# A gated mix of a state-space layer and an FFN: B turned by transposing transfers, ten FFN tiles ahead of the first Bu, one run of second FFN products

## The chip, the cores and the metric

The kernel runs on one core of one Trainium2 chip. The metric is the device time of one execution in microseconds (us). The core has five engines with instruction streams of their own: TensorE (PE in the profile, its weight loads PEld), VectorE (DVE), ScalarE (ACT), GpSimd (POOL) and SyncE (SP), which here only issues transfers (DMAs). KB is 1024 bytes.

## The reference

For each of 2048 tokens x has 448 features. Two branches are computed from it and mixed by a gate:

```python
g = sigmoid((x * gate_w).sum(-1, keepdims=True))
# branch a: a diagonal complex recurrence over the tokens
dt = exp(log_dt); Lam_bar = exp(dt * Lam)
B_bar = ((Lam_bar - 1) / Lam)[:, None] * (B_re + 1j * B_im)
Bu = x @ B_bar.T                        # 448 complex states for each token
h[t] = Lam_bar * h[t - 1] + Bu[t]
a = 2 * (h @ (C_re + 1j * C_im).T).real + x * Dskip
# branch b: an FFN
b = silu(x @ w1) @ w2                   # 448 -> 1792 -> 448
out = g * a + (1 - g) * b
```

## The kernel before

The tokens are cut into four chunks of 512. Four kinds of product on TensorE make up nearly all of its time:

- F(tc): the first FFN product of chunk tc, 14 tiles of 128 hidden features by 512 tokens. ScalarE evicts each from PSUM through Silu into `aT[tc % 2]`.
- B(tc): Bu of chunk tc, seven tiles ("slots") of 128 real numbers by 512 tokens. Slots 0 to 2 hold the real parts of states 0 to 383, slots 4 to 6 their imaginary parts, and slot 3 both parts of the last 64 states. They are evicted into `UG[tc % 3]`, by VectorE for chunk 0 and by ScalarE for the others. Slot 3 is also copied with its halves exchanged (two transfers from POOL, lines 681 to 683).
- G (`ffn2`, line 806): the second FFN product of a block of 128 tokens, 14 matmuls (L812). ScalarE scales the result by 1 - g (L818), and a POOL transfer adds it to `Tb` (L820), which holds x * Dskip * g.
- C (`readout`, line 824): the readout of a block of 128 tokens, seven matmuls (L833), then a VectorE operation that scales by g and adds `Tb` (L843), and a store from SP.

F and B are run by `x_products` (line 685). K is 448, so it is split into seven half-height pieces of 64 rows, and two tiles go side by side in the two halves of the array: one pair of tiles is 14 matmuls at L701. The first half of a pair (four steps) is issued ahead of the second half (three steps) of the pair before it. The `fill` argument puts other work behind a given pair, and `wait` turns the order of the two halves round for one pair.

Between B and C come the lanes (line 744) on VectorE: Bu is rotated by tables of cosine and sine, a real scan runs along the 512 tokens for each slot (L774), its result is cast by a POOL transfer (L407, UG<-Gf), and it is rotated back into `H`. A chunk's first scan starts from the last column of the chunk before. The tables and the scale of C are computed on the way (`parameters`, `readout_weights`).

[...] Chunk 0 of x is turned by TensorE (L513), chunks 1 to 3 by transposing transfers from SP (`turn`, L447), C too. B is loaded in rows into `UG[2]` (`Bnat`) and turned by TensorE (`b_transposes`, line 630, matmuls at L641, 64x64 pieces), in three calls for slots 0-1, 2-3 and 4-6. VectorE and ScalarE each copy one half of the result into `BT` (L649, L651).

The order of the work: TensorE's stream is that in which the code adds it. For the other engines a planner (`Plan.order`, line 120) lists the operations once, when the kernel is built, by estimated costs, times of landing and priorities; on the chip each engine follows that fixed list and waits on semaphores. SP's loads follow in the order in which they are added, since each gets the next number as its priority (`load`, `turn`). A load of w1 is cut by columns (`w1cuts`, line 409), and each cut goes as two transfers.

The order on TensorE before: eight tiles of F(0), B(0), the rest of F(0), B(1); G of tokens 0 to 511; F(1), one tile of F(2) and B(2); G of tokens 512 to 1023; the rest of F(2), B(3), F(3); then C and G to the end (lines 896 to 918).

Of the kernel before, what the change touches and what calls it, by code (L numbers as in the profile page):

```python
# [15 lines left out]
D_MOD = 448  # L16
F_FF = 1792
CH = 512
# [8 lines left out]
XT1K = 6  # L27
S0 = (0, 4, 1, 5, 2, 6, 3)
XT1 = "da"
XDMA = (1,2,3)  # L30
XAFT = ["PO1"]
UDVE = (0, 1, 2, 3, 4, 5, 6)
OUTA = (8, 9, 10, 11)
PRMF = (1, 0)
# [5 lines left out]
XCOL = [0, 128, 256, 320]  # L40
# [255 lines left out]
def bass_gated_mix__ssm_conv_s5__dense_activation_silu__prompt_kernel(nc, A_x, A_Lambda_re, A_Lambda_im, A_B_re, A_B_im, A_C_re, A_C_im,  # L296
               A_log_dt, A_Dskip, B_x, B_w1, B_w2, gate_w, out):
    with ExitStack() as ctx:
        E = ctx.enter_context
        P = Plan()  # L300

        def sb(name, shape, dtype):
            return E(nc.sbuf_tensor(name, list(shape), dtype))

        x2, out2 = A_x[0], out[0]

        xnat = sb("xnat", [128, NTB, D_MOD], BF16)
        xT = sb("xT", [128, NCH, 4, CH], BF16)
        w1s = sb("w1s", [128, 4, F_FF], BF16)
        w2s = sb("w2s", [128, NFB, D_MOD], BF16)  # L310
        BT = sb("BT", [128, 4, 896], BF16)
        CP = sb("CP", [128, NSLOT, CH], BF16)
# [9 lines left out]
        gwb = sb("gwb", [128, D_MOD], BF16)  # L322
        dkb = sb("dkb", [128, D_MOD], BF16)
# [5 lines left out]
        C3, c3n = ot[NOT - 1], " ".join(f"ot{NOT - 1}{m}" for m in range(3))  # L329
# [35 lines left out]
        g = sb("g", [128, NTB], F32)  # L365
# [5 lines left out]
        def sem():  # L371
            _s[0] += 1
            return E(nc.semaphore(name=f"d{_s[0]}"))

        def bk(t, k=0):
            return ps[:, t.bank + k, :]
# [25 lines left out]
        nl = [0]  # L402

        def load(q, dst, src, name, nbytes, prio=None, after=()):
            nl[0] += 1
            prio = nl[0] if prio is None else prio
            P.add(q, lambda e: e.dma_start(dst, src), list(after), name.split(), 0.6 if q == "pool" else 0.5 if nbytes > 2000 else 0.35, prio, sem(), nbytes, tag="ld " + name)  # L407

        w1cuts = [0, 256, 512, 1024, 1792]

        def load_w1(q, k, a, b):

            cols = slice(w1cuts[k], w1cuts[k + 1])
            n = cols.stop - cols.start
            if a == 3:
                src = B_w1[320:448, cols].rearrange("(b p) f -> p b f", p=128)
            elif b == 4:
                src = bass.AP(B_w1.tensor, 128 * a * F_FF + cols.start, [[F_FF, 128], [(320 - 128 * a) * F_FF, 2], [1, n]])
            else:
                src = B_w1[128 * a:128 * b, cols].rearrange("(b p) f -> p b f", p=128)  # L420
            load(q, w1s[:, a:b, cols], src, " ".join(f"w1_{k}_{i}" for i in range(a, b)), 256 * (b - a) * n)
# [2 lines left out]
            load(q, xnat[:, 2 * h:2 * h + 2, :], x2[256 * h:256 * h + 256, :].rearrange("(b p) d -> p b d", p=128), f"xn0{h}", 256 * 896)  # L424
        load_w1("sp", 0, 0, 2)
        load_w1("act", 0, 2, 4)
        for k in range(1, len(w1cuts) - 2):
            load_w1("sp", k, 0, 2)
            load_w1("sp", k, 2, 4)
        for k, v in enumerate((A_log_dt, A_Lambda_re, A_Lambda_im)):  # L430
            load("act", prm[k:k + 1, 0:448], v.rearrange("(o n) -> o n", o=1), f"prm{k}", 896, PRMP)
        Bnat = UG[2][:, :, 0:D_MOD]
        load("sp", Bnat[:, 0:3, :], A_B_re[0:384, :].rearrange("(b p) d -> p b d", p=128), "U2_0 U2_1 U2_2", 384 * 896)
        load("sp", Bnat[0:64, 3, :], A_B_re[384:448, :], "U2_3", 64 * 896)
        load("sp", Bnat[64:128, 3, :], A_B_im[384:448, :], "U2_3i", 64 * 896)
        load("sp", Bnat[:, 4:7, :], A_B_im[0:384, :].rearrange("(b p) d -> p b d", p=128), "U2_4 U2_5 U2_6", 384 * 896)
        btn = {s: [f"BT{s}_{h}" for h in range(2)] for s in range(7)}
        load_w1("sp", len(w1cuts) - 2, 0, 2)
        load_w1("sp", len(w1cuts) - 2, 2, 4)
        def load_xn(tc):  # L440
            load("sp", xnat[:, 4 * tc:4 * tc + 4, :],
                 x2[tc * CH:(tc + 1) * CH, :].rearrange("(b p) d -> p b d", p=128), f"xn{tc}", CH * 896)

        def turn(dst, src, name, nbytes, cost, after=()):

            nl[0] += 1
            P.add("sp", lambda e: e.dma_start_transpose(dst, src), list(after), name.split(), cost, nl[0], sem(), nbytes, tag="ldT " + name)  # L447

        def turn_x(tc, after=()):
            for c, n in ((0, 3), (3, 1)):  # L450
                turn(xT[:, tc, c:c + n, :], x2[tc * CH:(tc + 1) * CH, XCOL[c]:XCOL[c] + 128 * n], " ".join(f"xT{tc}_{q}" for q in range(c, c + n)), CH * 256 * n, 2.6 if n == 3 else 1.3, after)

        def turn_C():


            for k, a in enumerate((A_C_re, A_C_im)):
                turn(CP[:, 4 * k:4 * k + 3, 0:D_MOD], a[:, 0:384], " ".join(f"CT{4 * k + m}" for m in range(3)), 448 * 768, 1.5)
                turn((CP[:, 3, 0:D_MOD], C3[:, :])[k][:, None, :], a[:, 320:448], "CT3" if k == 0 else c3n, 448 * 256, 1.6)

        if 1 in XDMA:  # L460
            turn_x(1)
        for dst, src, name in ((gwb, gate_w, "gwb"), (dkb, A_Dskip, "dkb")):
            load("sp", dst[:, :], src.rearrange("(o n) -> o n", o=1).partition_broadcast(128).rearrange("p o n -> p (o n)"),
                 name, 128 * 896)
        if 1 not in XDMA:
            load_xn(1)
        load("sp", w2s[:, :, :], B_w2.rearrange("(fb p) d -> p fb d", p=128), "w2", F_FF * 896)
        if 2 in XDMA:
            turn_x(2)
        turn_C()  # L470
        if 3 in XDMA and not XAFT:
            turn_x(3)
        if 1 in XDMA:
            load_xn(1)
        load_xn(2)
        load_xn(3)

        POOL(lambda e: e.iota(idi, pattern=[[1, 128]], base=0, channel_multiplier=-1), [], ["PO1"], 0.3, 0)
        POOL(lambda e: e.tensor_single_scalar(ident[:, :], idi, 0, ALU.is_equal), ["PO1"], ["ident"], 0.5, 0)
# [50 lines left out]
        xn_of = {tc: {q: [f"xT{tc}_{h}" for h in range(2)] for q in range(4)} for tc in range(1, NCH)}  # L530
        for tc in XDMA:
            xn_of[tc] = {q: [f"xT{tc}_{q}"] for q in range(4)}
# [97 lines left out]
        def b_transposes(s0, s1, who):  # L630

            tk = Ps(2)
            n = s1 - s0

            def mm(pe):
                for i in range(4):
                    for q in range(n):
                        o = (i * n + q) * 64
                        for h in range(2):
                            p = slice(64 * h, 64 * h + 64)  # L640
                            r = pe.transpose(bk(tk, h).bitcast(BF16)[:, o:o + 64], Bnat[p, s0 + q, XCOL[i]:XCOL[i] + 128], ident[p, p])  # L641
                return r
            PE(mm, [f"U2_{s}" for s in range(s0, s1)] + ["U2_3i"] * (s0 <= 3 < s1) + ["ident"], [tk], n * 4 * 0.0285, "BT")
            for h in range(2):
                src = lambda h=h: bk(tk, h).bitcast(BF16)[:, 0:256 * n].rearrange("p (i s c) -> p i s c", i=4, s=n)
                dst = BT[:, :, :].rearrange("p i (s h c) -> p i s h c", h=2, c=64)[:, :, s0:s1, h, :]
                names = [f"BT{s}_{h}" for s in range(s0, s1)]
                if who[h] == "d":
                    DVE(lambda e, src=src, dst=dst: e.tensor_copy(dst, src()), [tk], names, 0.15 + n * 0.136, 2, "BTe")  # L649
                else:  # L650
                    ACT(lambda e, src=src, dst=dst: e.activation(dst, src(), AF.Copy), [tk], names, act_cost(256 * n), 2, "BTe")  # L651
# [83 lines left out]
        def F(tc, a=0, b=NFB):  # L735
            return [("F", tc, k) for k in range(a, b)]

        def B(tc):
            return [("B", tc, k) for k in ((3, 0, 4, 1, 5, 2, 6) if tc else (0, 1, 2, 3, 4, 5, 6))]
# [144 lines left out]
        def xt(tc, who):  # L884
            return [lambda: x_transposes(tc, who)]

        def cp(*slots):
            return [lambda k=k: readout_weights(k) for k in slots]

        def G(*tbs):  # L890
            return [lambda tb=tb: ffn2(tb) for tb in tbs]

        def C(*tbs):
            return [lambda tb=tb: readout(tb) for tb in tbs]

        turn_b = [lambda: b_transposes(0, 2, "da"), lambda: b_transposes(2, 4, "da"), lambda: b_transposes(4, 7, "da")]
        NH = 8
        K = NH // 2
        x_products(F(0, 0, NH) + B(0) + F(0, NH) + B(1),
                   {PRMF: [parameters], (K - 2, 0): turn_b[:1], K - 2: turn_b[1:2], K - 1: turn_b[2:], XT1K: xt(1, XT1) if 1 not in XDMA else [], 8: [lambda: lanes(0)] + [lambda: turn_x(3, XAFT)] * (3 in XDMA and bool(XAFT))}, [K - 2])  # L900
        gates(0)
        gates(1)
        lanes(1)
        for f in G(0, 1, 2, 3):
            f()
        for f in cp(0, 1, 2, 3):
            f()
        x_products(F(1) + F(2, 0, 1) + B(2), {2: xt(2, "aa")} if 2 not in XDMA else {})
        gates(2)
        lanes(2)  # L910
        for f in G(4, 5, 6, 7):
            f()
        x_products(F(2, 1) + B(3) + F(3), {1: xt(3, "aa") if 3 not in XDMA else [], 9: [lambda: gates(3)]})
        for f in C(0, 1, 2, 3):
            f()
        lanes(3)
# [37 lines left out]
```

## Time and profile before

| | |
|---|---|
| three runs | 138.43, 138.74, 138.75 us; median 138.74 |
| profiled execution | 139.01 us, of which the profile's span is 137.2 us |
| busy in the span | PE 133.7 us (97%), DVE 119.4 (87%), ACT 88.6 (65%), POOL 42.6 (31%) |
| L701, F | 392 matmuls, 48.1 us busy |
| L701, Bu | 196 matmuls, 25.8 us |
| L812, second FFN product | 224 matmuls, 43.0 us |
| L833, readout | 126 matmuls, 21.7 us |
| L641, turning B | 56 matmuls, 1.3 us |
| transfers | 16.78 MB, 122 GB/s in the mean |

Matmuls overlap in their pipeline, so the busy time of a group is more than what it adds to TensorE's time. The chain that ended last, followed back from the last instruction, gives each piece's own share. The share of transfers of SP's queue shows when each transfer was issued and how long that held the queue; "us to landing" is from the start of the issue to the arrival of its semaphore.

### The profile page before, as it was taken

To read this page: it belongs to the slowest core of one execution; us is meant where nothing else is said; L and a number is where in the kernel's file an instruction comes from. 1 tells how busy PE (TensorE), PEld (TensorE's weight loads), DVE (VectorE), ACT (ScalarE), POOL (GpSimd) and SP (SyncE) were. 2 spreads that over 40 slices of the span, in tenths; PEclk is the share of its full clock that TensorE was granted. 3 is DMA by queue.
4 is the path that set the end of the run, shared out by engine and by line. 5 is a ranking of instruction groups with operands and counts; after the bars stand their busy time and mean duration, and the time that the engine had idled before them with its cause. 6 is when DMAs were issued, how large, how long until landed. Compare 5 with 4: busy or idle time off the path is not lost.

```text
span 137.2 us, 2658 instructions
## 1 busy us (share of the span) xinstructions
PE 133.7 (97%) x1041; PEld 64.9 (47%) x1041; DVE 119.4 (87%) x161; ACT 88.6 (65%) x157; POOL 42.6 (31%) x76
## 2 busy tenths in 40 slices
PE   7999999999999999999999999999999999999991
PEld 2545444445544444455444444445555555555561
DVE  0418999999999999999999999999999999997053
ACT  3239757999436999897459999699401129782200
POOL 7224040110639403476410030723000420457310
DMA  4999799999969994568440010765331321239942
GB/s 131 339 339 200 142 273 219 162 200 213 262 132 146 167 107 101 80 95 132 74 75 0 0 43 0 99 95 91 92 104 57 79 41 26 33 63 117 196 99 68
DMA packets 26659, 16.78 MB, mean 122 GB/s; under 512 B 11923, under 2 KB 26518, under 8 KB 26646
## 3 DMA queue, kind: packets, MB, share of 16 engines
q1 hardware_dynamic: 19456, 10.28, 34.9%
q0 software_dynamic: 6640, 5.97, 29.0%
q10 hardware_dynamic: 550, 0.36, 0.8%
q8 instruction: 8, 0.13, 0.5%
q14 instruction: 5, 0.04, 0.1%
HBM read 6.31 MB, written 1.84 MB: 59 GB/s over the span
## 4 chain that ended last, share of the span: by engine, by line
PE 97%; DVE 0%; issue 0%
PE ps L701 47%; PE ps L812 31%; PE ps L833 16%; PE ps L498 2%; PE ps L513 1%; PE ps L641 1%; DVE ot L843 0%; PE ps L713 0%; PE ps L499 0%; PE ps L573 0%
## 5 line engine op out<-in xcount | busy, mean ns | idle before, releaser
L701 PE MATMUL ps<-xT,w1s 64*128 64x512 bf16 x392 | 48.1, 380 | 0.0
L812 PE MATMUL ps<-w2s,aT 128*128 128x448 bf16 x224 | 43.0, 353 | 0.0
L671 ACT ACTIVATE aT<-ps 128x1024 bf16<-128x1024 f32 (+1 forms) x30 | 28.8, 964 | 9.3 <-PE ps L701 9.1
L812 PEld LDWEIGHTS ps<-w2s,aT 128*128 128x128 bf16 x224 | 21.8, 98 | 20.9 <-issue 0.4
L701 PEld LDWEIGHTS ps<-xT,w1s 64*128 64x128 bf16 x392 | 20.2, 95 | 23.1 <-issue 0.8
L701 PE MATMUL ps<-xT,BT 64*128 64x512 bf16 x196 | 25.8, 376 | 0.0
L774 DVE TENSOR_TENSOR_SCAN Gf<-rc,gin,H 128x512 f32<-128x512 f32 x21 | 25.5, 1269 | 0.1
L820 POOL DMA_DIRECT2D xnat<-fe x16 | 14.4, 899 | 35.9 <-ACT fe L818 29.6
L818 ACT ACTIVATE fe<-ps,g 128x448 bf16<-128x448 f32 x16 | 10.1, 630 | 20.5 <-PE ps L812 16.6
L833 PE MATMUL ps<-CP,H 128*128 128x448 bf16 (+2 forms) x126 | 21.7, 332 | 0.0
L407 POOL DMA_DIRECT2D UG<-Gf x27 | 15.9, 734 | 15.5 <-DVE Gf L774 15.3
L833 PEld LDWEIGHTS ps<-CP,H 128*128 128x128 bf16 x126 | 11.6, 98 | 10.0 <-issue 0.4
L742 DVE TENSOR_TENSOR H<-UG,COS 128x3584 bf16<-128x3584 bf16 (+2 forms) x9 | 16.2, 1814 | 0.0
L701 PEld LDWEIGHTS ps<-xT,BT 64*128 64x128 bf16 x196 | 10.8, 94 | 11.2 <-DVE Gf L599 0.2
L407 POOL DMA_DIRECT2D UG<-UG x8 | 4.7, 596 | 30.8 <-ACT UG L680 24.1
L843 DVE SCALAR_TENSOR_TENSOR ot<-ps,g,xnat 128x448 bf16<-128x448 f32 (+2 forms) x14 | 8.2, 614 | 5.7 <-issue 4.4
L680 ACT ACTIVATE UG<-ps 128x1024 bf16<-128x1024 f32 (+1 forms) x12 | 10.6, 920 | 0.0
L874 ACT ACTIVATE junk<-xg 128x448 bf16<-128x448 bf16 x16 | 9.2, 574 | 1.8 <-DVE xg L742 1.7
L881 ACT ACTIVATE xnat<-xnat,g 128x448 bf16<-128x448 bf16 x16 | 9.9, 666 | 0.1
L742 DVE TENSOR_TENSOR PO<-UG,SIN 128x1536 bf16<-128x1536 bf16 (+1 forms) x8 | 8.6, 1086 | 0.2 <-DMA UG<-Gf 0.2
L742 DVE TENSOR_TENSOR PI<-UG,SIN 128x1536 bf16<-128x1536 bf16 (+1 forms) x8 | 8.5, 1083 | 0.0
L742 DVE TENSOR_TENSOR H<-H,PI 128x3584 bf16<-128x3584 bf16 x4 | 8.1, 2022 | 0.1
(93 smaller groups left out, 100.6 us busy)
## 6 DMA issues: line engine op xcount, KB each, us to landing
UG<-Gf POOLq DMA_DIRECT2D x21, 128.0 KB, 2.7
xnat<-fe POOLq DMA_DIRECT2D x16, 112.0 KB, 2.6
w2s<-in_B_w_dram SPq DMA_DIRECT2D x1, 1568.0 KB, 10.1
xnat<-in_A_x_dram SPq DMA_DIRECT2D x3, 448.0 KB, 6.1
out_dram<-ot SPq DMA_DIRECT2D x11, 112.0 KB, 1.7
w1s<-in_B_w_dram SPq DMA_DIRECT2D x2, 384.0 KB, 5.9
w1s<-in_B_w_dram SPq DMA_DIRECT2D x2, 256.0 KB, 4.0
UG<-UG POOLq DMA_DIRECT2D x8, 64.0 KB, 2.2
```

The source lines that it names most:

```text
L407: P.add(q, lambda e: e.dma_start(dst, src), list(after), name.split(), 0.6 if q == "pool" else 0.5 if nbytes > 2000 else 0.35, prio, sem() ...
L671: ACT(lambda e, src=src, dst=dst: e.activation(dst, src(), AF.Silu), [tk, "tbl"], [f"aT{tc % 2}_{m}" for m in names], act_cost(512 * n), 2 ...
L680: ACT(lambda e, src=src, dst=dst: e.activation(dst, src(), AF.Copy), [tk], after, act_cost(512 * n), 5, "U")
L701: r = pe.matmul(bk(toks[k], b), weights(tile, p0, p0 + 64, i), xT[p0:p0 + 64, tc, i, :], start=(h == 0 and n == 0), stop=(h == 1 and n == 2))
L742: DVE(lambda e: e.tensor_tensor(o, a, b, op), r, w, dve_cost(n, 2), prio, tag)
L774: DVE(lambda e, s=s, b=b, init=init: e.tensor_tensor_scan(Gf[:, s, :], rc[:, b:b + 1].to_broadcast([128, CH]), A[:, s, :], init, ALU.mult, ...
L812: r = pe.matmul(bk(tk)[:, 0:D_MOD], aT[tc % 2][:, fb, o:o + 128], w2s[:, fb, :], start=(fb == 0), stop=(fb == NFB - 1))
L818: ACT(lambda e: e.activation(f[:, :], bk(tk)[:, 0:D_MOD], AF.Copy, scale=g1[:, tb:tb + 1]), [tk, f"g1_{tc}"], [fn], act_cost(448, 1), 7, "fe")
L820: P.add("pool", lambda e: e.dma_start(Tb[:, tb, :], f[:, :], accum_op=ALU.add), [fn, f"Tb{tb}"], [f"Tb{tb}"], 0.94, 2, sem(), 250000, tag= ...
L833: r = pe.matmul(bk(tk)[:, 0:b - a], H[tc % 3][:, s, o:o + 128], CP[:, s, a:b], start=(s == 0), stop=(s == NSLOT - 1))
L874: ACT(lambda e, tb=tb, b=b: e.activation(junk[:, :], xg[:, b, :], AF.Copy, accum_out=zl[:, tb:tb + 1]), ["xg"], ["junk", f"zl{tc}"], act_c ...
L881: ACT(lambda e, tb=tb: e.activation(Tb[:, tb, :], xnat[:, tb, :], AF.Copy, scale=g[:, tb:tb + 1]), [f"xd{tc}", f"g_{tc}"], [f"Tb{tb}"], ac ...
```

## The change

Five of B's seven slots are loaded by transposing transfers straight into `BT`; slots 0 and 1 are still loaded in rows and turned by TensorE. The list `LORD` gives the new order of the loads on SP. w1 is cut into five column ranges, not four. Ten tiles of F(0) precede B(0). The two runs of G for tokens 0 to 1023 become one; ahead of it stand F(1) and six slots of B(2), behind it three tiles of F(2), the last slot (3) of B(2), and the rest as before. The planner's costs of transposing transfers and their rate are changed, as is the place where `lanes(2)` and `gates(3)` are added to its list.

```diff
-XDMA = (1,2,3)
+LORD = "B2 w3 BH B3 BI w4 x1 g n1 w2 x2 C n2 n3".split()
+BPE = ((0,2),)
+TRATE = 2
+MERGE = True
+NHF = 10
+MB = 6
+MP = 3
+GAT = 10
+W1CUTS = [0,256,512,1024,1280,1792]
+L2AT = 1
...
-        for k in range(1, len(w1cuts) - 2):
+        for k in range(1, 3):
             load_w1("sp", k, 0, 2)
             load_w1("sp", k, 2, 4)
...
+        def turn_B(a, r0, r1, to, slots):
+            for c, n in ((0, 3), (3, 1)):
+                names = [f"BT{s}T{c}_{to}" for s in slots]
+                for s, m in zip(slots, names):
+                    btn[s] = (btn[s] if s == 3 or c else []) + [m]
+                turn(BT[:, c:c + n, to:to + r1 - r0], a[r0:r1, XCOL[c]:XCOL[c] + 128 * n], " ".join(names), (r1 - r0) * 256 * n, 0.7 + 0.0042 * n * (r1 - r0) / 4 * 1.0)
...
+        do = {
+            "w3": lambda: [load_w1("sp", 3, r, r + 2) for r in (0, 2)],
+            "w4": lambda: [load_w1("sp", 4, r, r + 2) for r in (0, 2)],
+            "B2": lambda: rows_B(A_B_re, 0, 0, 2, 0),
+            "BH": lambda: turn_B(A_B_re, 256, 448, 256, (2, 3)),
+            "B3": lambda: turn_B(A_B_im, 384, 448, 448, (3,)),
+            "BI": lambda: turn_B(A_B_im, 0, 384, 512, (4, 5, 6)),
+            "g": rows_g,
...
+            "x1": lambda: turn_x(1), "x2": lambda: turn_x(2), "C": turn_C,
+            "n1": lambda: load_xn(1), "n2": lambda: load_xn(2), "n3": lambda: load_xn(3),
+        }
+        for k in LORD:
+            do[k]()
...
-        turn_b = [lambda: b_transposes(0, 2, "da"), lambda: b_transposes(2, 4, "da"), lambda: b_transposes(4, 7, "da")]
-        NH = 8
+        turn_b = [lambda a=a, z=z: b_transposes(a, z, "da") for a, z in BPE]
+        NH = NHF
...
+            b2 = B(2)[1:] + B(2)[:1]
+            for f in cp(0, 1, 2, 3):
+                f()
+            x_products(F(1) + b2[:MB], {})
+            gates(2)
+            for f in G(0, 1, 2, 3, 4, 5, 6, 7):
+                f()
+            x_products(F(2, 0, MP) + b2[MB:] + F(2, MP) + B(3) + F(3), {L2AT: [lambda: lanes(2)], GAT: [lambda: gates(3)]})
```

A transposing transfer is issued once for the first three blocks of 128 columns and once for the last (`(0, 3), (3, 1)`), so B's five slots take six of them: 192, 64 and 384 rows, twice each. The order before, on SP after the first w1 loads: B in four loads, the last w1 columns, x of chunk 1 turned, gate_w and Dskip, w2, x of chunk 2 turned, C turned, the rows of chunks 1 to 3 of x.

More of the change, by code (lines that the diff above doesn't have):

```diff
@@ L29 @@
 XT1 = "da"
-XDMA = (1,2,3)
+XDMA = (1, 2, 3)
 XAFT = ["PO1"]
+LORD = "B2 w3 BH B3 BI w4 x1 g n1 w2 x2 C n2 n3".split()
[8 more added lines that the diff above has]
+L2AT = 1
 UDVE = (0, 1, 2, 3, 4, 5, 6)
@@ L407, in load @@
             P.add(q, lambda e: e.dma_start(dst, src), list(after), name.split(), 0.6 if q == "pool" else 0.5 if nbytes > 2000 else 0.35, prio, sem(), nbytes, tag="ld " + name)
-        w1cuts = [0, 256, 512, 1024, 1792]
+        w1cuts = W1CUTS
         def load_w1(q, k, a, b):
@@ L432, in bass_gated_mix__ssm_conv_s5__dense_activation_silu__prompt_kernel @@
         Bnat = UG[2][:, :, 0:D_MOD]
[L433 to L436, printed above, removed]
         btn = {s: [f"BT{s}_{h}" for h in range(2)] for s in range(7)}
-        load_w1("sp", len(w1cuts) - 2, 0, 2)
-        load_w1("sp", len(w1cuts) - 2, 2, 4)
         def load_xn(tc):
@@ L446, in turn @@
             nl[0] += 1
-            P.add("sp", lambda e: e.dma_start_transpose(dst, src), list(after), name.split(), cost, nl[0], sem(), nbytes, tag="ldT " + name)
+            P.add("sp", lambda e: e.dma_start_transpose(dst, src), list(after), name.split(), cost, nl[0], sem(), TRATE * nbytes, tag="ldT " + name)
         def turn_x(tc, after=()):
             for c, n in ((0, 3), (3, 1)):
-                turn(xT[:, tc, c:c + n, :], x2[tc * CH:(tc + 1) * CH, XCOL[c]:XCOL[c] + 128 * n], " ".join(f"xT{tc}_{q}" for q in range(c, c + n)), CH * 256 * n, 2.6 if n == 3 else 1.3, after)
+                turn(xT[:, tc, c:c + n, :], x2[tc * CH:(tc + 1) * CH, XCOL[c]:XCOL[c] + 128 * n], " ".join(f"xT{tc}_{q}" for q in range(c, c + n)), CH * 256 * n, 3.9 if n == 3 else 1.4, after)
@@ L453, in turn_C @@
         def turn_C():
             for k, a in enumerate((A_C_re, A_C_im)):
[L457 to L476, printed above, removed]
+                turn(CP[:, 4 * k:4 * k + 3, 0:D_MOD], a[:, 0:384], " ".join(f"CT{4 * k + m}" for m in range(3)), 448 * 768, 2.3)
+                turn((CP[:, 3, 0:D_MOD], C3[:, :])[k][:, None, :], a[:, 320:448], "CT3" if k == 0 else c3n, 448 * 256, 1.3)
@@ new lines, in turn_B, with rows_B @@
+        def turn_B(a, r0, r1, to, slots):
[4 more added lines that the diff above has]
+                turn(BT[:, c:c + n, to:to + r1 - r0], a[r0:r1, XCOL[c]:XCOL[c] + 128 * n], " ".join(names), (r1 - r0) * 256 * n, 0.7 + 0.0042 * n * (r1 - r0) / 4 * 1.0)
+        def rows_B(a, r0, s0, s1, p0):
+            if s1 - s0 > 1:
+                load("sp", Bnat[:, s0:s1, :], a[r0:r0 + 128 * (s1 - s0), :].rearrange("(b p) d -> p b d", p=128), " ".join(f"U2_{s}" for s in range(s0, s1)), 128 * (s1 - s0) * 896)
+            else:
+                load("sp", Bnat[p0:p0 + 64, s0, :], a[r0:r0 + 64, :], f"U2_{s0}" + "i" * (p0 == 64), 64 * 896)
@@ new lines, in rows_g @@
+        def rows_g():
+            for dst, src, name in ((gwb, gate_w, "gwb"), (dkb, A_Dskip, "dkb")):
+                load("sp", dst[:, :], src.rearrange("(o n) -> o n", o=1).partition_broadcast(128).rearrange("p o n -> p (o n)"),
+                     name, 128 * 896)
+        do = {
+            "w1": lambda: [load_w1("sp", k, r, r + 2) for k in range(3, len(w1cuts) - 1) for r in (0, 2)],
+            "w3": lambda: [load_w1("sp", 3, r, r + 2) for r in (0, 2)],
+            "w4": lambda: [load_w1("sp", 4, r, r + 2) for r in (0, 2)],
+            "Br": lambda: (rows_B(A_B_re, 0, 0, 3, 0), rows_B(A_B_re, 384, 3, 4, 0), rows_B(A_B_im, 384, 3, 4, 64)),
+            "Bi": lambda: rows_B(A_B_im, 0, 4, 7, 0),
+            "B2": lambda: rows_B(A_B_re, 0, 0, 2, 0),
+            "BR": lambda: turn_B(A_B_re, 0, 448, 0, (0, 1, 2, 3)),
+            "BH": lambda: turn_B(A_B_re, 256, 448, 256, (2, 3)),
+            "B3": lambda: turn_B(A_B_im, 384, 448, 448, (3,)),
+            "BI": lambda: turn_B(A_B_im, 0, 384, 512, (4, 5, 6)),
+            "g": rows_g,
+            "w2": lambda: load("sp", w2s[:, :, :], B_w2.rearrange("(fb p) d -> p fb d", p=128), "w2", F_FF * 896),
+            "x1": lambda: turn_x(1), "x2": lambda: turn_x(2), "C": turn_C,
+            "n1": lambda: load_xn(1), "n2": lambda: load_xn(2), "n3": lambda: load_xn(3),
+        }
@@ L903, in bass_gated_mix__ssm_conv_s5__dense_activation_silu__prompt_kernel @@
         lanes(1)
[L904 to L913, printed above, removed]
+        if MERGE:
+            b2 = B(2)[1:] + B(2)[:1]
[6 more added lines that the diff above has]
+            x_products(F(2, 0, MP) + b2[MB:] + F(2, MP) + B(3) + F(3), {L2AT: [lambda: lanes(2)], GAT: [lambda: gates(3)]})
+        else:
+            for f in G(0, 1, 2, 3):
+                f()
+            for f in cp(0, 1, 2, 3):
+                f()
+            x_products(F(1) + F(2, 0, 1) + B(2), {2: xt(2, "aa")} if 2 not in XDMA else {})
+            gates(2)
+            lanes(2)
+            for f in G(4, 5, 6, 7):
+                f()
+            x_products(F(2, 1) + B(3) + F(3), {1: xt(3, "aa") if 3 not in XDMA else [], 9: [lambda: gates(3)]})
         for f in C(0, 1, 2, 3):
```

## The prediction, as it was put on record

> **What bounds the kernel now.** I read the chain that ended last first. It is TensorE from 0.76 us to 134.47 us, 97% of the span, and no stretch of it waits. The granted clock is 1.00 in every stretch of 2 us that I asked for up to 34 us. So the time is the sum of TensorE's pieces, and an edit counts in two ways only: by the pieces that it takes out, and by any gap that it opens. In the chain the columns are start, length, and what ran:
>
> ```profile
> PE 97%; DVE 0%; issue 0%
> ```
> ```profile
> 9.19 1.62 PE ps L701 x14
> 10.81 0.23 PE ps L641 x16
> 11.04 0.65 PE ps L701 x6
> 11.69 0.23 PE ps L641 x16
> 11.93 1.51 PE ps L701 x14
> 13.44 0.35 PE ps L641 x24
> ...
> 28.03 10.70 PE ps L812 x56
> 38.73 16.73 PE ps L701 x154
> 55.45 10.70 PE ps L812 x56
> 66.15 25.79 PE ps L701 x238
> ```
>
> The reader is to see three things. L641, the turning of B on TensorE, costs 0.23 + 0.23 + 0.35 = 0.81 us. A pair of 64-row matmuls at L701 costs 1.51 / 7 = 0.2157 us, so a pair of tiles is 0.86 us (first half, four steps) + 0.65 us (second half, three). And a change of matmul form has a price: 16.73 us less 77 x 0.2157 is 0.12 us, 25.79 us less 119 x 0.2157 is also 0.12, and 10.70 us less 56 x 0.189 (the full-height 448-column step of line 46; the long run of 84 gives 15.89 / 84 = 0.1892) is 0.11.
>
> Second, SP's queue, since the change gives it six more transfers of the kind that L447 issues. Columns: start, time on SP's queue, what was issued:
>
> ```profile
> 6.16 1.00 SPq L407 DMA_DIRECT2D w1s<-in_B_w_dram  x2
> 7.20 5.43 SPq L447 DMA_TRANSPOSE xT<-in_A_x_dram  x2
> ...
> 15.00 9.52 SPq L447 DMA_TRANSPOSE xT<-in_A_x_dram  x2
> 24.56 3.57 SPq L447 DMA_TRANSPOSE CP<-in_A_C_re_dram  x2
> 28.17 1.52 SPq L447 DMA_TRANSPOSE CP<-in_A_C_im_dram  x1
> 29.73 1.33 SPq L447 DMA_TRANSPOSE ot<-in_A_C_im_dram  x1
> ```
>
> A plain load holds SP for 0.5 us, a transposing one never under 1.26 us. By narrower windows the first 7.20 entry is 3.88 us (three blocks, 512x384) and 1.51 us (one block); at 15.00 it is 8.22 and 1.26. The long ones end about when the plain loads ahead have drained: at 11.08 us, where the traffic falls from 340 GB/s at about 11.2 us, and at 23.22 us, behind w2.
>
> Third, VectorE, whose last scan work decides when the last readout can start:
>
> ```profile
> 124.04 2.09 DVE L742 TENSOR_TENSOR H<-H,PO 128x2048 bf16<-128x2048 bf16 x2
> 130.55 0.68 DVE L843 SCALAR_TENSOR_TENSOR ot<-ps,g,xnat 128x448 bf16<-128x448 f32 x1 [4.41 <-issue]
> ```
>
> H is done at 126.13 us; its readout (PE L833) begins at 128.97 us. VectorE, busy all the way before, has 2.84 us of cover.
>
> **Part 1: B by transfer.** Five of seven slots no longer pass through TensorE: L641 keeps one call of 16 transposes (0.23 us) and loses the other two, 0.23 + 0.35 = **0.58 us off the chain**. VectorE loses copies of 0.41 and 0.55 us, ScalarE 0.59 and 0.83 us; neither is on the chain, so they count as cover only (VectorE 0.96 us).
>
> **Part 2: one run of second products.** The sequence L701, L812, L701, L812, L701 becomes L701, L812, L701. One change each way disappears: 0.11 + 0.12 = **0.23 us off**. The number of matmuls is the same (28 pairs of tiles after token 511's products, split 10 + 18 where it was 11 + 17). So 0.81 us, if no gap opens.
>
> **Part 3: ten FFN tiles first.** This adds no work, one pair moves ahead. The first Bu start was 12.41 us; it moves by 1.51 less the 0.23 that no longer precedes it, to 13.69. From there the needs follow by the pair: slots 2 and 3 at 13.69 + 0.86 = 14.55, slots 4 to 6 at 16.06, the last two w1 loads (tile 10) at 17.57, the turned x of chunk 1 at 20.6 us (before: 21.18, in the list of PE's work, less 0.58). Tiles 8 and 9 need w1's columns 1024 to 1279 at about 11.3.
>
> **Part 4: do the transfers arrive?** The loads through 1472 KB landed at 7.38 us, through 2256 KB at 9.93 us, through 3024 KB at 12.79 us. In the new order 1952 KB (B's first two slots and w1's columns 1024 to 1279 last) come ahead of any transpose: by interpolation they land at 8.9 us, and tiles 8, 9 and slots 0, 1 have over 2 us of cover. SP issues the first turned part of B at 3.80 + 3 x 0.51 = 5.33 us. Six B transposes (192, 64 and 384 rows, three blocks and one block each), two w1 loads, and the two of x follow, all in SP's order.
>
> No row shows a transpose of so few rows. Bounds for its time on SP: from below 0.44 us, w2's plain issue; from above 1.28 to 1.33 us (448 rows, one block) and 1.52 us (448 rows, three), with the first held until the loads drain at 8.0. From 448 to 512 rows nothing grows (1.28 against 1.26), which speaks for the upper end; the planner's edited costs (0.77 to 1.9 us) are guesses of the code, not rows. I take 1.0 us on average, a little nearer the upper rows than the lower one, and the first one held to 7.2 us, midway between 6.5 (not held) and 8.0. Then B's last transpose leaves SP at about 12.6 us. One block of 448 rows landed 1.8 to 3.1 us after its issue ended (31.06 to 32.9; 28.13 to 31.25), which gives 14.4 to 15.7 us, inside the 16.06 needed. The w1 loads go at 12.7 and 13.2; 256 KB loads landed in 3.9 to 4.1 us at full traffic, so 17.3 against 17.57. Chunk 1 of x is issued at 13.75, is held by 512 KB of w1 to about 15.6, its second part leaves at 16.9; that part landed 3.5 to 3.7 us after its issue ended in all three chunks (12.64 to 16.13; 24.52 to 28.26; 50.57 to 54.3). So **20.5 us against 20.6**, and the weight load leads the matmul by 0.2 us (12.20 and 12.41 us at the first Bu): a gap of 0.1 us. At the lower end there is none. At the upper end the last B part leaves SP at 14.65, x's second part at 18.5, lands at 22.1, and the gap is 1.6 us.
>
> [...]
>
> **Part 5: the rest of the moved work.** w2, x's chunk 2, C and the last natural rows are issued some 5 us later than before; w2 lands near 30 us, needed at 42.5 (28.03 - 0.58 + ten pairs of 1.51), C near 38 us, needed at 58.8, x's chunk 2 near 33, needed at 64. gate_w and Dskip land near 21 and 23.5 us against uses at 23.77 and 24.95: cover 1.4 us, then VectorE's own. F(1) now runs at 27.5 to 38 beside the gates of chunk 0: ScalarE must evict ten pairs at 1.02 us in 15.1 us, and a pair may be evicted 2.0 us late (four pairs fit in PSUM: 3.02 less 1.02); the gates' 6 us slip into the run of second products, where ScalarE has 0.64 us of work in each 2.65. The eight accumulating POOL transfers (0.9 us each) now stand at 45 to 64 and no longer beside the casts of chunk 0 (36.6 to 46). The last slot of chunk 2's Bu is ready at about 71 us, its lanes begin at 75.00. I cost all of this at nothing. If the covers go, VectorE is late first: beyond 2.84 - 0.7 + 0.96 = 3.1 us, one for one.
>
> **Sum.** 139.01 us is the profiled execution (span 137.2 and 1.8 around it): 139.01 - 0.58 - 0.23 + 0.1 = 138.3. The median shown is 0.27 lower: 138.74 - 0.71 = **138.0 us**.
>
> **Rivals.**
> - *SP's queue is dear, and the time is about the same.* If a small transpose costs nearly what a large one does, x's chunk 1 lands at 21.0 to 21.8, the gap is 0.4 to 1.2 us and eats the gain: 138.3 to 139.15. For it: no transpose in the trace is under 1.26 us. Against it: all of these have 448 or 512 rows, these have 64 to 384.
> - *The same mechanism in full, slower.* Place: the first pair that needs x's chunk 1. Price: one for one with its landing after 20.6. It decides from 21.4 us on, and shows beyond 21.8: each transpose at 1.28 to 1.5 us and the first held till the loads drain give 22.1 and 139.5; with B's last part landing 3.2 to 4.4 us after its start, slots 4 to 6 are late by 0.6 to 1.7 us as well, which lies inside the same gap. For it: both long transposes behind plain loads were held until these drained. Against it: those were 1536 rows-by-blocks long, this one is 576. [...]
> - *VectorE becomes the bound.* Its order is fixed by the planner; if casts of Bu, gate_w and Dskip come later than planned it idles, beyond 3.1 us the last readout waits: 138.8 to 140. Against it: three covers must fail together.
> - *The change of form costs the same however often.* If the 0.11 and 0.12 are starts that reappear elsewhere, 0.58 us alone remains: 138.25.
>
> **How the numbers follow.** Forecast, gap under 0.4 us (137.9 to 138.3): 0.50. Same-size gap: 0.24. Full gap: 0.14. VectorE: 0.06. No gain from the form: 0.06. A measurement of this kernel tells 0.3%, 0.42 us, from no change. Faster beyond that: 0.50 and two thirds of the last, 0.54. Within: 0.24 + 0.03 = 0.27. Slower: 0.14 + 0.05 = 0.19. The range runs from 137.75 (the full 0.81 and the 0.2 us by which runs of the same kernel differ) to 139.6, past the full gap's 139.5.
>
> **What would show it.** In the chain after: one L641 piece of x16, one L812 piece of 112 matmuls of about 21.3 us, and L701 pieces at 0.2157 us a pair between 13.7 and 42 us. A gap would stand ahead of the first matmul that mixes w1 and BT after 20 us, or ahead of slots 4 to 6 near 16 us, put down to a transfer. SP's list shows at once what a transpose of 64 or 192 rows holds. I am wrong if that is 1.3 us throughout, or if VectorE's last H ends after 128 us.

## The result, and the profile after

The changed kernel took 140.36 us (median of five runs, 140.14 to 140.61) against 138.64 us for the kernel before (median of five, 138.43 to 138.75): a ratio of 1.0105, 95% interval 1.0078 to 1.0133. It is slower by 1.7 us. The forecast was 138.0 us and the range ended at 139.6.

The profiled execution took 140.61 us with a span of 138.7. In this kernel L701 is L726, L812 is L837, L833 is L858, L641 is L666, L407 is L417, L447 is L452. TensorE's own list shows where the time came from. Columns: start, time, what ran, and in brackets the idle time before it:

```profile
12.02 0.40 PE L666 MATMUL ps<-ident,UG 64*128 64x64 bf16 x16
...
13.55 4.05 PE L726 MATMUL ps<-xT,BT 64*128 64x512 bf16 x36
18.75 0.37 PE L726 MATMUL ps<-xT,BT 64*128 64x512 bf16 x1 [1.15 <-ACT SIN L622]
...
43.67 21.36 PE L837 MATMUL ps<-w2s,aT 128*128 128x448 bf16 x112
...
68.65 0.38 PE L726 MATMUL ps<-xT,w1s 64*128 64x512 bf16 x1
69.99 6.43 PE L726 MATMUL ps<-xT,w1s 64*128 64x512 bf16 x57 [0.96 <-ACT aT L696]
```

One call of 16 turns of B is left, and the second products are one run. There are two gaps. 36 matmuls (18 pairs) from 13.55 us should have ended the pattern at 13.55 + 18 x 0.2157 = 17.43 us; the next pair starts at 18.75, so the first gap is 1.32 us. The second is 69.99 - 68.65 - 0.22 = 1.12 us. The idle time in brackets (1.15 and 0.96 us) is shorter because it counts from the end of the matmul before, which the profile draws 0.38 us long, while the next of the pattern starts 0.22 us after it. The account closes: 139.01 - 0.81 + 1.32 + 1.12 = 140.64 us, against 140.61 measured. That it closes to 0.03 us is in part chance. In the spans the same sum gives 138.83 us against 138.7; TensorE began Bu at 13.55 us and not at the 13.69 of the forecast, which accounts for the difference. So the pieces came off the chain as forecast, and two gaps gave back three times as much.

The first gap's label (a sine on ScalarE) is only the last releaser that the profile saw. The matmuls that wait are the first to read FFN tile 10, whose weights are w1's last columns. The profile of ct_early, an experiment below that leaves these loads as they are, puts the same gap down to them:

```profile
18.68 0.37 PE L726 MATMUL ps<-xT,BT 64*128 64x512 bf16 x1 [0.75 <-DMA w1s<-in_B_w_dram]
```

SP's queue in the change shows when they went:

```profile
5.33 2.55 SPq L452 DMA_TRANSPOSE BT<-in_A_B_re_dram  x2
7.92 5.96 SPq L452 DMA_TRANSPOSE BT<-in_A_B_im_dram  x4
13.93 1.09 SPq L417 DMA_DIRECT2D w1s<-in_B_w_dram  x2
15.07 3.69 SPq L452 DMA_TRANSPOSE xT<-in_A_x_dram  x2
...
38.94 1.20 SPq L417 DMA_DIRECT2D xnat<-in_A_x_dram  x2
```

Six transposes of B hold SP for 8.5 us, and each one-block one takes 1.22 to 1.25 us, whether it carries 96 KB (384 rows) or 16 KB (64 rows). The second of w1's last two loads is issued at 14.56 and lands 4.0 us later, at 18.56.

The second gap is a longer chain. First VectorE's list, then ScalarE's:

```profile
47.06 0.96 DVE L767 TENSOR_TENSOR PO<-UG,SIN 128x1536 bf16<-128x1536 bf16 x1 [2.31 <-DMA UG<-Gf]
...
58.07 7.16 DVE L799 TENSOR_TENSOR_SCAN Gf<-rc,gin,H 128x512 f32<-128x512 f32 x6
65.15 4.35 DVE L887 SCALAR_TENSOR_TENSOR CP<-CP,sc1s,ct 128x448 bf16<-128x448 bf16 x7
```
```profile
62.03 0.66 ACT L885 ACTIVATE ct<-CP,scc 128x448 f32<-128x448 bf16 x1
65.85 0.67 ACT L884 ACTIVATE ct<-CP,scc 128x448 f32<-128x448 bf16 x1 [3.16 <-DVE CP L887]
...
68.38 0.63 ACT L843 ACTIVATE fe<-ps,g 128x448 bf16<-128x448 f32 x1
68.92 1.50 ACT L696 ACTIVATE aT<-ps 128x1024 bf16<-128x1024 f32 x2
```

VectorE waits 2.31 us for the cast of a scan of chunk 0. Its scans of chunk 1 then start at 58.07 us, and the copies CP of C only follow at 65.15. ScalarE's fixed list has the fifth product ct of C at this place; it needs a buffer that the first CP frees, and waits 3.16 us. Behind it stand the eviction of the seventh of the eight second products (68.38) and those of F(2) (68.92), due when TensorE began F(2) at 64.97. TensorE has to wait for the first eviction of F(2) (`0.96 <-ACT aT L696`, above). The planner had the first CP at 61 us and the first eviction of F(2) at 66 us.

The cast that VectorE waits for is the fifth, of slot 2. POOL issued it at 41.24 us, and it took 5.7 us to land (46.94):

```profile
41.24 0.53 POOL L417 DMA_DIRECT2D UG<-Gf  x1 [0.59 <-DVE Gf L799]
```
```profile
UG<-Gf POOLq DMA_DIRECT2D x1, 128.0 KB, 5.7
```

Why it was late: the one before it took 6.2 us, and from 39 to 46 us the core moved 200 to 360 GB/s, because the rows of chunks 2 and 3 of x (896 KB) were issued at 38.94 us. In the kernel before they were the last two of three loads, at 31.7 and 32.3 us, and VectorE's wait for a cast was 0.2 us:

```profile
31.11 3.84 SPq L407 DMA_DIRECT2D xnat<-in_A_x_dram  x3
```
```profile
DVE PO L742 <- DMA UG<-Gf: 0.2, 1, 0.2
```

That these rows are the cause is tested below (late_rows).

### The profile page after: what moved, and what is told of

It is laid out like the page before. It is cut to its first block, busy times and chain, and to the rows that moved or that the text cites. A ratio compares the mean times of both kernels' runs of the same rounds, so it can differ in the third digit from the quotient of the medians.

```text
span 138.7 us, 2575 instructions
## 1 busy us (share of the span) xinstructions
PE 133.1 (96%) x1001; PEld 66.2 (48%) x1001; DVE 118.7 (86%) x159; ACT 86.9 (63%) x155; POOL 42.0 (30%) x76
## 4 chain that ended last, share of the span: by engine, by line
PE 89%; DVE 6%; ACT 2%; POOL 1%; issue 0%
PE ps L726 40%; PE ps L837 31%; PE ps L858 15%; PE ps L523 2%; DVE Gf L589 1%; DVE Gf L617 1%; DVE UG L703 1%; POOL dtc L605 1%; DVE Gf L586 1%; PE ps L538 1%; ACT aT L696 1%; DVE Gf L624 0%; ACT SIN L622 0%; ACT fe L843 0%; DVE BT L674 0%
## 5 line engine op out<-in xcount | busy, mean ns | idle before, releaser
L726 PE MATMUL ps<-xT,w1s 64*128 64x512 bf16 x392 | 48.2, 380 | 1.0 <-ACT aT L696 1.0
L837 PE MATMUL ps<-w2s,aT 128*128 128x448 bf16 x224 | 42.9, 353 | 0.0
L696 ACT ACTIVATE aT<-ps 128x1024 bf16<-128x1024 f32 (+1 forms) x30 | 28.5, 961 | 8.0 <-PE ps L726 8.0
L726 PEld LDWEIGHTS ps<-xT,w1s 64*128 64x128 bf16 x392 | 21.2, 95 | 23.3 <-ACT aT L696 1.5
L837 PEld LDWEIGHTS ps<-w2s,aT 128*128 128x128 bf16 x224 | 21.8, 98 | 20.7 <-issue 0.4
L726 PE MATMUL ps<-xT,BT 64*128 64x512 bf16 x196 | 26.0, 376 | 1.2 <-ACT SIN L622 1.2
L845 POOL DMA_DIRECT2D xnat<-fe x16 | 13.9, 870 | 35.4 <-ACT fe L843 35.4
L417 POOL DMA_DIRECT2D UG<-Gf x27 | 15.0, 559 | 27.7 <-DVE Gf L799 27.3
L858 PE MATMUL ps<-CP,H 128*128 128x448 bf16 (+2 forms) x126 | 21.7, 332 | 0.0
L726 PEld LDWEIGHTS ps<-xT,BT 64*128 64x128 bf16 x196 | 11.5, 94 | 12.0 <-ACT SIN L622 1.8
L858 PEld LDWEIGHTS ps<-CP,H 128*128 128x128 bf16 x126 | 11.6, 98 | 10.0 <-DVE xnat L767 0.4
L417 POOL DMA_DIRECT2D UG<-UG x8 | 4.9, 615 | 21.3 <-ACT UG L705 13.7
```

The source lines that it names most:

```text
L726: r = pe.matmul(bk(toks[k], b), weights(tile, p0, p0 + 64, i), xT[p0:p0 + 64, tc, i, :], start=(h == 0 and n == 0), stop=(h == 1 and n == 2))
L837: r = pe.matmul(bk(tk)[:, 0:D_MOD], aT[tc % 2][:, fb, o:o + 128], w2s[:, fb, :], start=(fb == 0), stop=(fb == NFB - 1))
L845: P.add("pool", lambda e: e.dma_start(Tb[:, tb, :], f[:, :], accum_op=ALU.add), [fn, f"Tb{tb}"], [f"Tb{tb}"], 0.94, 2, sem(), 250000, tag= ...
L858: r = pe.matmul(bk(tk)[:, 0:b - a], H[tc % 3][:, s, o:o + 128], CP[:, s, a:b], start=(s == 0), stop=(s == NSLOT - 1))
```

## The experiments

They ran on three chips: w4_act, ct_early, two_runs and merge_only on one, late_rows, bi_only, bi_late and full12 on another, the last two on a third. Each ratio is to the kernel before on the same chip. There it had medians of 138.9 to 139.1 us, and the runs compared spread by 0.9 to 1.3 per cent; so the intervals of the ratios are wide, and I read the mechanisms from the spans and pieces of the profiles, one profile for each kernel. The profiled span of the kernel before is 137.2 us, that of the change 138.7.

**w4_act: w1's last columns from another queue.**

```diff
-            "w4": lambda: [load_w1("sp", 4, r, r + 2) for r in (0, 2)],
+            "w4": lambda: [setattr(load_w1("act", 4, r, r + 2), "at", 5.2) for r in (0, 2)],
```

(`load` and `load_w1` return the operation, so that its earliest planned time can be set.)

> The changed kernel with one edit: the last two loads of w1 (columns 1280 to 1791) are issued by ScalarE at about 5.2 us instead of by SP behind B's six transposes. Every engine's list is otherwise the same. Theory A (the first gap, 1.32 us ahead of the first pair that mixes Bu's slot 6 and FFN tile 10, waits for w1's last columns): that gap goes, the next need is x's chunk 1, which then leaves SP 1.1 us earlier, so no new gap; 140.36 - 1.3 = about 139.05 us, second gap still there near 68 us. Rival A1 (the gap waits for B's last transposes, slot 6 being in the same pair): gap and time stay, 140.2 to 140.4. Rival A2 (it waits for PSUM or ScalarE, as the trace's label SIN says): also unchanged.

Measured: ratio 0.9989 (0.9962 to 1.0016), span 137.3. The first gap moved and named its cause:

```profile
PE ps L726 <- DMA BT<-in_A_B_im_dram: 0.7, 1, 0.7
```

TensorE now waits until 16.78 us for the last transpose of B, which lands at 16.64 (12.13 + 4.51; in the change 15.73). By the pattern it was due at 13.54 + 11 x 0.2157 = 15.91 us, so a gap of 0.87 us stands in place of the 1.32. Why this transpose took 4.5 us and not the 3.1 of the change is not shown: the load of w1 that ScalarE issued between 5 and 6 us landed 5.7 us later, ahead of this transpose, and from 12.2 to 13 us the core moved 164 GB/s. So the gap of the change was w1's (A), and B's last slots stood right behind it: with w1 out of the way they become the bound. That no new gap would open was a miss, and so was the second gap, forecast to stay and now gone: the rows of x left SP at 35.37 us, 3.6 us earlier than in the change, VectorE's wait fell from 2.31 to 1.29 us, and ScalarE's wait for CP (2.14 us) now ended in time: TensorE has no wait for an eviction. The forecast of 1.3 us less is near the 1.4 us by which the span fell (138.7 to 137.3) only because these two misses offset each other.

**ct_early: the products of C planned earlier.**

```diff
-CTAT = 59.0
+CTAT = 50.0
```

> The changed kernel with CTAT 59 made 50: ScalarE's eight products ct of C, each pair of which waits for VectorE's CP to free its buffer, are planned inside the run of second FFN products. Theory B (the second gap, 1.12 us near 69 us, comes from ScalarE's fixed list: ct waits for VectorE, which runs some 4 us behind the plan, and behind ct stand the evictions that PSUM needs): the gap goes, 140.36 - 1.1 = about 139.25 us; the first gap near 17.5 us stays at 1.3. Rival B1 (ScalarE has simply too much work after the merged run, or the last slot of Bu of chunk 2 is what PE waits for): gap stays, 140.2 to 140.4.

Measured: ratio 1.0075 (1.0035 to 1.0116), span 138.4. The time is a miss. The gap at 69 us went, but another opened: with seven of the eight CP copies now ahead of its scans and the eighth behind the first scan, VectorE reached the gate products of chunk 2 at 71.14 us, ScalarE's list waited for these 2.15 us, and TensorE stood before 73.87 and again before 81.7 us. From the start of F(2) to that of the first readout (64.90 to 93.04 us) it is 28.14 us, against 28.43 in the change and 27.30 without a gap: of the 1.1 us only 0.3 were regained. Theory B was right that ScalarE's list hands VectorE's lateness to TensorE; moving one item only made the next one late. What had to be removed was the lateness.

**two_runs: the loads and the ten tiles without the merged run.**

```diff
-MERGE = True
+MERGE = False
```

> The changed kernel with MERGE off: B by transfer and ten FFN tiles first, but second FFN products in two runs as before. By the pieces: 138.64 - 0.58 + 1.3 (first gap) = 139.35 us if the second gap belongs to the merged run; up to 140.4 if VectorE's lateness alone makes it.

Measured: ratio 1.0325 (1.0257 to 1.0393), span 141.4: a miss. With the second products at 28 us again, w2 is late. It is issued at 20.28 us, not at 14.51, and lands at 30.5:

```profile
PE ps L837 <- DMA w2s<-in_B_w_dram: 2.1, 1, 2.1
```
```profile
30.00:32.00 2.00, 1.49 (x5) 0.65 (x6) 2.00 (x2) 1.89 (x7) 0.00 (x0) 0.69 1.27 201
32.00:34.00 2.00, 2.00 (x6) 0.73 (x5) 2.00 (x2) 0.30 (x2) 0.00 (x0) 0.50 1.26 92
34.00:36.00 2.00, 2.00 (x12) 1.04 (x11) 1.97 (x2) 0.89 (x2) 0.00 (x0) 0.96 1.01 214
```

The second fence has stretches of 2 us; the third number from the right is the granted clock. After the idle 2.1 us it is 0.69, 0.50 and 0.96 in these stretches, and the first run of 56 takes 12.45 us in place of 10.70. So the merged run of the change also gave the late w2 the time that it needed. No second gap is in this profile, though VectorE's wait for a cast is (2.3 us, as in the change). Lateness of VectorE alone did not make the second gap here; but TensorE, too, was 4 us later at that place (its run of 238 starts at 70.38 us, before at 66.15), so this run does not separate the two.

**merge_only: the merged run on the loads of before.**

```diff
-LORD = "B2 w3 BH B3 BI w4 x1 g n1 w2 x2 C n2 n3".split()
-BPE = ((0,2),)
+LORD = "Br Bi w1 x1 g w2 x2 C n1 n2 n3".split()
+BPE = ((0, 2), (2, 4), (4, 7))
-NHF = 10
+NHF = 8
-W1CUTS = [0,256,512,1024,1280,1792]
+W1CUTS = [0, 256, 512, 1024, 1792]
```

> The kernel before with the merged run alone (loads, eight FFN tiles ahead and B's turning on TensorE as before). No first gap. By the pieces 138.64 - 0.23 = 138.4 us without a second gap; 139.5 us if the merged run makes the second gap by itself.

Measured: ratio 0.9989 (0.9946 to 1.0033), span 137.0. The pieces are those expected: one run of 21.29 us between stretches of 29.35 and 27.30 us with no gap, 0.2 us off the span. The casts of 128 KB land in 2.2 to 2.3 us. The merged run alone does not make the second gap.

**late_rows: the rows of chunks 2 and 3 behind the turned x of chunk 3.**

```diff
-LORD = "B2 w3 BH B3 BI w4 x1 g n1 w2 x2 C n2 n3".split()
+LORD = "B2 w3 BH B3 BI w4 x1 g n1 w2 x2 C".split()
...
-[lambda: turn_x(3, XAFT)] * (3 in XDMA and bool(XAFT))
+[lambda: turn_x(3, XAFT), lambda: load_xn(2, XAFT), lambda: load_xn(3, XAFT)]
```

(`load_xn` hands `after` on to `load`.)

> The changed kernel with one edit: the natural rows of x's chunks 2 and 3 are issued by SP behind the turned x of chunk 3 (about 51 us) instead of behind C (38.9 us); every other engine's list is the same. Theory C (these 896 KB, pushed to 39 to 46 us by SP's longer queue, run beside the casts of chunk 0's scans and make them land in 5 to 6 us instead of 2.3; VectorE waits 2.3 us for one of them, is late, and through ScalarE's list causes the second gap): casts land in under 3 us, the 2.3 us wait is gone or under 0.3, the second gap (1.1 us near 69) goes, the first stays: span 138.7 - 1.1 = 137.6 us. Rival (the casts are slow because of POOL's own queue or the second gap comes from the first): wait and gap stay, span 138.5 to 138.7.

Measured: ratio 1.0014 (0.9996 to 1.0033), span 137.5. The pieces of the chain (start, length):

```profile
18.66 25.00 PE ps L726 x230
43.66 21.29 PE ps L837 x112
64.95 27.30 PE ps L726 x252
```

27.30 us for 252 matmuls is 126 x 0.2157 and one change of form: the second gap is gone, with every other engine's list the same. VectorE no longer waits for a cast. That the casts would land in under 3 us was a miss: those issued at 40 and 42 us took 4.0 and 3.0 us, the first one 5.0, with C's transposes beside it. But the fifth, for which VectorE had waited 2.31 us, was issued between these two and no longer kept it waiting. So Theory C holds in what it says of the rows and the second gap. The first gap is there, ending at 18.66 us, and with it VectorE's wait of 1.0 us for a Bu tile; that wait alone made no second gap.

**bi_only, bi_late, full12: versions without the gaps.** bi_only takes slots 2 and 3 of B back to rows and TensorE; bi_late adds the late rows; full12 keeps all five slots by transfer, puts twelve FFN tiles ahead of Bu and w1's last columns ahead of B's transposes, and has the late rows. For bi_only:

```diff
-LORD = "B2 w3 BH B3 BI w4 x1 g n1 w2 x2 C n2 n3".split()
-BPE = ((0,2),)
+LORD = "Br w3 BI w4 x1 g n1 w2 x2 C n2 n3".split()
+BPE = ((0, 2), (2, 4))
```

For full12, beside the edit of late_rows:

```diff
-LORD = "B2 w3 BH B3 BI w4 x1 g n1 w2 x2 C".split()
+LORD = "B2 w3 w4 BH B3 BI x1 g n1 w2 x2 C".split()
-NHF = 10
+NHF = 12
-8: [lambda: lanes(0)]
+K + 3: [lambda: lanes(0)]
```

> Slots 2 and 3 of B go back to rows and TensorE (one more call of 16 transposes, 0.23 us); only the imaginary part of states 0 to 383 comes by two transposing transfers, so SP issues two of them and not six ahead of w1's last columns. If each transposing transfer holds SP some 1.25 us whatever its size, w1's last columns leave SP some 3.5 us earlier and the first gap goes: span 137.2 - 0.35 - 0.23 = 136.6 us, plus up to 1.1 if the late rows of x still disturb the casts. If the gap comes from the DMA traffic and not from SP's issue time, it stays at about 1 us.

> Both edits together (only two transposes of B, rows of chunks 2 and 3 late). By the theories no gap is left: span 137.2 - 0.58 = 136.6 us, and 138.64 - 0.58 = 138.1 us on a quiet chip, 0.4% under the kernel before.

> All five slots of B by transfer as in the change, but twelve FFN tiles ahead of the first Bu, w1's last columns ahead of B's transposes on SP, rows of chunks 2 and 3 late. By the theories the needs of slots 4 to 6 move to 17.6 us, which they meet (landing near 16.8), and w1 is early; x's chunk 1 lands near 20.6 against 20.4: span 137.2 - 0.81 + 0.2 = 136.6 us. If B's transposes come later behind the extra 512 KB, a gap of up to 1 us near 17 us stays.

Measured: bi_only 0.9951 (0.9927 to 0.9976), span 136.5; bi_late 0.9974 (0.9947 to 1.0001), span 136.7; full12 0.9963 (0.9946 to 0.9981), span 136.3. In bi_only SP issues w1's last columns at 9.83 us, 4.1 us earlier, and TensorE does not wait after that. Its casts of 128 KB land in 4.1 us at 36 us (median of two) and in 2.3 at 42, and VectorE waits for none, so the late rows of bi_late have nothing left to mend. The chain of full12:

```profile
13.74 0.23 PE ps L666 x16
13.97 28.49 PE ps L726 x264
42.46 21.29 PE ps L837 x112
63.76 27.30 PE ps L726 x252
```

264 matmuls in 28.49 us are 132 x 0.2157 and no more. The span is 0.9 us under that of before.

**full12_5 and bi_only_5: the same two, timed longer.**

> The same kernel as full12, timed longer: by its pieces (0.58 + 0.23 us off the chain, no gap but the early one of w1 that the kernel before has too) 138.64 - 0.81 = 137.8 us on a quiet chip, a ratio of 0.994; a ratio above 0.998 would say that something outside the chain takes the gain.

> The same kernel as bi_only, timed longer beside full12: it keeps 0.23 us of turning on TensorE, so it should be 0.2 us slower than full12, ratio 0.996; if it is not slower, the four further transposing transfers bring nothing.

Measured: full12 138.16 us against 138.91, ratio 0.9931 (0.9907 to 0.9955); bi_only 138.38, ratio 0.9957 (0.9937 to 0.9976). The two medians stand 0.2 us apart, in the order expected, but the intervals overlap, so that order is not shown. Both are faster than the kernel before, by 0.7 and 0.4 per cent, and by these ratios than the change (1.0105), which was not timed on this chip.

## Why the prediction was wrong

- **Parts 1 and 2, the pieces: right.** 0.58 and 0.23 us came off; full12's span, with both and without a gap, is 0.9 us shorter, and merge_only's 0.2 us, as near to 0.11 + 0.12 us as single profiles tell. What TensorE does in the 0.11 and 0.12 us of a change of form is not shown.
- **Part 4, the price of a small transpose: the step that failed first.** I took 1.0 us on average, though the rows, as I said, spoke for more. Measured: one-block ones 1.22 to 1.25 us, those of three blocks 1.28 (192 rows), 1.24 (64) and 2.12 (384), all six in 8.5 us, where the sum put 7.3. The first was not held until the loads drained: the next went at 6.66 us and not at 7.2, which hid 0.5 us of the error. The other five took 7.2 us where the sum had 5.4. My reading that a plain load holds SP for 0.5 us left out two of the same list, Dskip (1.16 us) and the last rows of x (2.67 us); the sum does not rest on them. My sign of being wrong, 1.3 us throughout, all but came: five of six took 1.22 to 1.28 us. B's last transpose left SP at 13.88 and not at 12.6, and w1's last columns went at 13.93 and 14.56, not at 12.7 and 13.2.
- **Part 4, who is late first: wrong.** I put the whole risk on x's chunk 1 and gave w1's last columns 0.3 us of cover, by a landing of 4 us that was right. They came 1.3 us later than I had them, at 18.56 us against 17.3. TensorE was ready for them at 17.43 us, a little before the 17.57 of the forecast, and started 0.2 us after the landing: the gap of 1.32 us. x's chunk 1 landed at 17.50 + 3.0 = 20.5 us, the time forecast, but by luck: its second part left SP at 18.76 us and not at 16.9, and landed 1.7 us after that and not 3.6. Behind the gap TensorE did not wait for it. B's last part landed at 15.73, in time.
- **Part 5, moved loads counted by their own due time only: the step that failed second.** I noted that the rows of x are issued later, priced the moved loads by when each is needed, and put the rows' effect on others at nothing. I did not ask what runs beside them in their new place, and counted the casts of chunk 0 as freer, since the accumulating POOL transfers move away from them. Those of 128 KB took 3.1 to 4.6 us in the kernel before and 2.2 to 2.3 us in merge_only; in the change they took 3.6 to 6.2 us, and VectorE waited 2.31 us for one. late_rows shows that the rows' new place made the second gap.
- **Part 5, VectorE's cover of 3.1 us: the wrong place.** I measured VectorE's lateness against the last readout only. That cover held (its H ends at 128.45 us, the readout begins at 130.49). But ScalarE's fixed list waits for VectorE in the middle of the kernel, and there VectorE's waits, 2.31 us for the cast and 1.06 us for a Bu tile in the first gap, were enough; without the first of them, in late_rows, there was no second gap. The other sign of being wrong, a last H after 128 us, came true as well: VectorE's H was 2.3 us later than before, but TensorE was 1.5 us later itself and did not wait for it. My second rival had the mechanism, SP's queue at full price, with the wrong first victim; its 139.5 us lacked the second gap, and so the range ended too low.

## What to carry to other kernels

When transfers are moved, price each by the time that it holds its issuing queue, not by its bytes alone (here 1.23 us for a transposing one of 16 KB, 1.25 us for one of 96 KB), and list the need of every load behind it; the one with the least cover is the first victim. Then ask what each displaced load will run beside in its new place, above all another queue's transfers that an engine waits for closely. In a kernel with fixed engine lists, an engine off the chain has covers at every place where another engine's list waits for it, not only at the end.

## What the runs showed of the hardware

- A transposing transfer of 64 rows by 128 columns (16 KB) held SP for 1.23 us (the change); one of 448 or 512 rows by 128 columns held it for 1.26 to 1.51 us in the kernel before, and for 1.26 to 2.75 us in the change.
- Casting transfers of 128 KB from POOL landed in 2.2 to 2.3 us where the core moved 3 to 131 GB/s (merge_only, bi_late, stretches of 1 us from 36 to 43 us). Beside loads of 448 KB from SP they took 4.8 to 6.2 us in the change (227 to 364 GB/s from 39 to 44 us), and with C's transposes beside them up to 5.0 us in late_rows.
- TensorE idle for 1.12 and 1.32 us kept a granted clock of 1.00 (the change, stretches of 2 us from 17 to 21 and from 69 to 73 us). After it was idle for 2.1 us the granted clock was 0.69, 0.50 and 0.96 in the three stretches of 2 us from 30 to 36 us (two_runs), at a further price of 12.45 - 10.70 = 1.75 us. That the idle time is the cause is read from the order of events in this one profile; of the four executions three had a mean granted clock of 0.988 and one 0.997, so it did not always come to this.
